# A gated linear attention feeding a gated MLP: the states of the first ten units from one scan each, and units five and six in 64-token chunks

## The chip, the core and the metric

The kernel is one program on 1 core of one Trainium2 chip. The metric is the device time of the program in microseconds (us); lower is better.

The engines have short names below. PE is TensorE's matmul and PEld its weight load. DVE is VectorE, ACT is ScalarE, POOL is GpSimd, and SP is SyncE, which here issues nearly all DMAs.

## The reference

```python
def _attn_ref(q, k, v, alpha):            # 4 x 8 heads, 768 tokens, 48 channels
    for t in range(S):
        state = alpha[:, :, t, :, None] * state + np.einsum('bhd,bhe->bhde', k[:, :, t], v[:, :, t])
        y[:, :, t] = np.einsum('bhd,bhde->bhe', q[:, :, t], state)

def _moe_ref(x, w_gate, w_val, w_out):    # x 3072 x 384, hidden 1536
    gate = 1.0 / (1.0 + np.exp(-(x @ w_gate)))
    val = x @ w_val
    return gate * val @ w_out
```

The output of the recurrence, with the heads side by side, is the `x` of the MLP. All is float32.

## The kernel before

**Units.** The 3072 tokens are cut into six groups `g` of T = 512. In a group, the eight heads are taken as four pairs `p`, so there are 24 units `u = 4 g + p`. A unit computes 512 tokens of two heads. Channels lie on the partitions: one head from partition 0, the other from partition 64.

**One unit.** DVE scans the decays into `G` (L418) and `F` (L422), and `k` and `q` are multiplied by them: L426 and L506 or L638, on DVE or POOL by the tables `KEYS`, `QUERIES` and `WHOLE`. `dec` (L424) holds one decay per chunk. PE transposes the scaled k (L439) and ACT copies it to `kn` (L443). PE computes scores within the chunks, which DVE masks into `A`, and one 48 x 48 addition to the state per chunk. The state is then carried from chunk to chunk: `st[c+1] = st[c] * dec[c] + addition[c]`, one DVE instruction per chunk (L546, L683). POOL multiplies the chunks' states by `dec` into `vs` (L584, L557, L690). PE then forms the outputs from states and scores.

**Two kinds of unit.** Units below `EARLY` = 6 have four chunks of C = 128 tokens (function `unit`). The others have eight chunks of E = 64 (function `late`). The four units of group 0 write their output straight into the PSUM banks `po` (function `in_place`, L597 from states and L602 from scores). Three casts on ACT (L610) and three subtractions on DVE (L611) then make the MLP's input of group 0 from them: `x` in a high and a low part, for k = 0, 1, 2.

**The MLP.** Each group goes through 12 steps, 72 in all. A step has 18 matmuls of 512 columns for gate and value (L245) and 9 into `po` (L746). Between them ACT computes the sigmoid `sg` (L734), DVE the product (L736), ACT its high part `hh` (L737) and DVE the rest `hl` (L738). In group 0, step f also needs weight piece f. It comes as packed words, and for each half of it ACT casts (L376), DVE merges (L379), ACT casts the high part (L382) and DVE subtracts the low part (L390).

**Who sets the order.** Every piece of work is an entry of a plan with an engine, an estimated time and what it reads and writes. For the early program the order on each engine is a table of entry numbers (`ORDER`); behind its end a planner goes by due times. Each engine then runs its own queue in that order. PE starts with 29 matmuls without use (L713).

Of the kernel before, what the change touches and what calls it, by code (L numbers as in the profile page):

```python
# [38 lines left out]
EARLY = 6  # L39
# [166 lines left out]
def act(n):  # L206
    return 0.01 + n / 1065
# [41 lines left out]
def chunked(ctx, tc, rows, vc, vh, vg, weights_in, out, const, ident, flags, weights, within):  # L249
# [64 lines left out]
    r_G0, r_dec = ring("G0", 2, EH), ring("dec", 4, EH)  # L314
# [96 lines left out]
    def decays(u, size, t, inn, tin):  # L411
# [5 lines left out]
        G0, dec = G0[:, 0:nch], dec[:, 0:nch]  # L417
# [11 lines left out]
        return fn, F, decn, dec, gn, G  # L429
# [55 lines left out]
    def unit(u, g, p, t):  # L485
# [6 lines left out]
        if g:  # L492
            vn, v = r_v.next()
            plan.add("sync", (0.475, P * CH * 2 * D * 4 / RATE), after(t["load"], 0.2), lambda: nc.sync.dma_start(
                out=v.rearrange("p c j e -> p (c j e)"), in_=vc[g, p]), writes=[(vn, "v")])
        else:
            vn, vw = r_vg.next()
            plan.add("sync", (0.475, P * CH * GAP * 4 / RATE), t["load"] if u else -1500.0, lambda: nc.sync.dma_start(
                out=vw.rearrange("p c e -> p (c e)"), in_=vg[p]), writes=[(vn, "v")])
            v = vw.rearrange("p c (o e) -> p c o e", o=1)  # L500
            v = [vw[:, :, R * j:R * j + D] for j in range(2)]
        vj = (lambda c, j: v[:, c, j]) if g else (lambda c, j: v[j][:, c])
# [8 lines left out]
        (pkn, pk), *pas = [r_bank.next() for _ in range(3)] if u < NP else [r_gv.next(), r_at.next(), r_at.next()]  # L511
# [26 lines left out]
        st, sn = sts[p], ("st", p)  # L538
        if g:
            plan.add("gpsimd", 0.18, t["G"], lambda: nc.gpsimd.tensor_copy(out=st[:, 0, :], in_=st[:, nch, :]), writes=[sn])  # L540
        else:
            plan.add("gpsimd", 0.08, t["G"], lambda: nc.gpsimd.memset(st[:, 0, :], 0.0), writes=[sn], port=False)

        def states(lo, hi):
            for c in range(lo, hi):
                nc.vector.scalar_tensor_tensor(out=st[:, c + 1, :], in0=st[:, c, :], scalar=dec[:, c:c + 1],  # L546
                                               in1=pk[:, c * D:(c + 1) * D], op0=ALU.mult, op1=ALU.add)

        some = min(t["run"], nch)
        for lo in range(0, nch, some):  # L550
            plan.add("vector", (0.3 * some - 0.12) if some > 1 else 0.19, t["S"], lambda lo=lo: states(lo, min(nch, lo + some)), [decn, pkn], [sn])
        sdn, sd = r_vs.next()
        if not g:
            in_place(p, t, qT, inn, (vn, vw), (an, A), (sdn, sd), (st, sn), (dec, decn))
            return
        sd = sd[:, 0, 0:CH, :]
        plan.add("gpsimd", 0.57, t["sd"], lambda: nc.gpsimd.tensor_tensor(  # L557
            out=sd, in0=st[:, 0:nch], in1=dec.rearrange("p (c o) -> p c o", o=1).broadcast_to([P, nch, D]), op=ALU.mult), [sn, decn], [(sdn, x) for x in range(4)])

        yield  # L560

        pyn, py = r_gv.next()

        def outputs():
            for c in range(nch):
                for j in range(2):
                    cs, r = slice(c * C, (c + 1) * C), slice(R * j, R * j + D)
                    nc.tensor.matmul(out=py[r, cs], lhsT=sd[r, c, :], rhs=qT[r, cs], start=(c == 0), stop=False)  # L568
            for c in range(nch):
                for j in range(2):  # L570
                    cs = slice(c * C, (c + 1) * C)
                    nc.tensor.matmul(out=py[R * j:R * j + D, cs], lhsT=v[:, c, j], rhs=A[:, j, cs],  # L572
                                     start=False, stop=(c == nch - 1))

        plan.add("tensor", (0.46 * nch + 0.15, 0.5), t["out"], outputs, [(vn, "v"), (inn, "q"), *((sdn, x) for x in range(4)), *((an, x) for x in range(4))], [pyn])
        finish(g, p, t, pyn, py)

    def in_place(p, t, qT, inn, vw, A, sd, st, dec):

        (vn, vw), (an, A), (sdn, sd), (st, sn), (dec, decn) = vw, A, sd, st, dec  # L580
# [23 lines left out]
        plan.add("tensor", (1.0, 0.5), t["out"], from_states, [(inn, "q"), *((sdn, x) for x in range(4))], banks)  # L604
# [208 lines left out]
    next(now), next(now)  # L813
# [39 lines left out]
CASTS = ((10, 0),)  # L853
QUERIES = (0, 2)
WHOLE = (4, 5, 6, 8, 9)
KEYS = (0, 1, 2, 3, 4, 8, 10)
# [207 lines left out]
```

## Time and profile before

| | us |
|---|---|
| median of three runs | 513.33 (512.8 to 513.36) |
| the profiled execution's own time | 512.68 |
| its span, first to last instruction | 510.9 |
| busy: PE, DVE, ACT, POOL | 500.6, 328.4, 172.5, 86.1 |

The span is 1.8 us shorter than the time of the same execution. Busy time of PE counts matmuls that overlap in its pipeline, so it is read together with the waits: an engine that is busy and waits for nobody sets the pace.

### The profile page before, as it was taken

The page shows a single profiled execution, that of the slowest core. Times are in us where ns is not written, and L with a number is a line of the kernel's source. Part 1 is how long each engine was busy: PE and PEld are TensorE (multiplying, and loading weights), DVE is VectorE, ACT ScalarE, POOL GpSimd, SP SyncE. Part 2 cuts the span into 40 slices and gives each one's busy share as a digit, 9 for nine tenths or more (in the row PEclk, how much of TensorE's full clock was granted, in tenths as well). Part 3 has the DMA queues.
Part 4 walks back from the last instruction along what each step waited for, and adds up shares of the span by engine and source line. Part 5 has one row for each costly group of instructions (what it writes and reads, how often), then busy time and mean ns, then how long its engine had stood idle before and what let it go on. Part 6 is the DMA issues. An engine that isn't in the chain of part 4 may idle for free.

```text
span 510.9 us, 10507 instructions
## 1 busy us (share of the span) xinstructions
PE 500.6 (98%) x4223; PEld 427.8 (84%) x4223; DVE 328.4 (64%) x639; ACT 172.5 (34%) x330; POOL 86.1 (17%) x110
## 2 busy tenths in 40 slices
PE   8899999999999999999999999999999999999995
PEld 4688888888888888888888888888888888888884
DVE  7999999987747768657558659568665442222221
ACT  2358556553323233223232323222332222311221
POOL 4353111302103303303203113012021010000000
PEclk9999999999999999999999999999999999999998
DMA  8857777851366535725625736436643000100001
GB/s 295 301 205 232 233 260 257 247 154 63 48 146 177 130 86 128 184 61 153 124 55 151 188 67 152 103 89 152 158 96 73 8 10 17 62 1 0 1 1 65
DMA packets 80677, 63.00 MB, mean 123 GB/s; under 512 B 61936, under 2 KB 67312, under 8 KB 80624
## 3 DMA queue, kind: packets, MB, share of 16 engines
q1 hardware_dynamic: 80624, 62.28, 45.2%
q8 instruction: 34, 0.56, 0.5%
q14 instruction: 19, 0.16, 0.1%
HBM read 45.22 MB, written 8.39 MB: 105 GB/s over the span
## 4 chain that ended last, share of the span: by engine, by line
PE 94%; DVE 4%; ACT 1%; DMA 1%; issue 0%; DVEq 0%; SPq 0%; ACTq 0%
PE gv L245 54%; PE po L746 28%; PE gv L702 4%; PE at L654 2%; PE at L660 1%; PE po L602 1%; DVE G L418 1%; PE at L518 1%; PE gv L439 1%; PE po L597 1%; DMA in<-in_rows_dram 1%; DVE raw L379 0%; PE gv L568 0%; PE gv L572 0%; PE gv L523 0%
## 5 line engine op out<-in xcount | busy, mean ns | idle before, releaser
L245 PE MATMUL gv<-x,w 128*128 128x512 f32 x1296 | 300.7, 380 | 0.2 <-DVE hl L738 0.2
L245 PEld LDWEIGHTS gv<-x,w 128*128 128x128 f32 x1296 | 244.4, 189 | 35.2 <-DVE hl L738 0.4
L736 DVE TENSOR_TENSOR gv<-gv,sg 128x512 f32<-128x512 f32 x72 | 50.1, 696 | 127.0 <-PE gv L245 124.1
L746 PE MATMUL po<-hh,w 128*128 128x512 f32 x432 | 111.4, 384 | 0.0
L746 PEld LDWEIGHTS po<-hh,w 128*128 128x128 f32 x432 | 79.9, 189 | 11.8
L734 ACT ACTIVATE sg<-gv 128x512 f32<-128x512 f32 x72 | 43.0, 597 | 127.8 <-PE gv L245 126.6
L737 ACT CAST hh<-gv 128x512 fp32r<-128x512 f32 x72 | 42.2, 586 | 124.1 <-DVE gv L736 114.3
L690 POOL TENSOR_TENSOR vs<-st,dec 64x384 f32<-64x384 f32 x36 | 37.1, 1031 | 270.2 <-PE gv L245 204.3
L738 DVE TENSOR_TENSOR hl<-gv,hh 128x512 fp32r<-128x512 f32 x72 | 49.0, 681 | 24.9 <-ACT hh L737 21.5
L746 PE MATMUL po<-hl,w 128*128 128x512 f32 x216 | 62.8, 381 | 0.0
L746 PEld LDWEIGHTS po<-hl,w 128*128 128x128 f32 x216 | 40.8, 189 | 6.0 <-issue 0.2
L683 DVE SCALAR_TENSOR_TENSOR st<-st,dec,at 128x48 f32<-128x48 f32 x144 | 37.9, 263 | 4.5
L418 DVE TENSOR_TENSOR_SCAN G<-in,d1g 128x512 f32<-128x512 f32 x22 | 31.5, 1431 | 8.7 <-DMA in<-in_rows_dram 8.1
L670 DVE TENSOR_TENSOR A<-at,mask 64x256 f32<-64x256 f32 x72 | 30.2, 420 | 3.5 <-PE at L660 2.8
L422 DVE TENSOR_TENSOR_SCAN F<-in,d1f 128x512 f32<-128x512 f32 x22 | 26.7, 1214 | 0.0
L426 POOL TENSOR_TENSOR in<-in,G 128x512 f32<-128x512 f32 x17 | 22.5, 1323 | 15.8 <-DVE G L418 11.8
L702 PE MATMUL gv<-A,vs 128*48 128x64 f32 x576 | 19.8, 221 | 0.0
L702 PEld LDWEIGHTS gv<-A,vs 128*48 128x48 f32 x576 | 17.1, 123 | 2.4 <-issue 1.3
L464 ACT COPY yt<-gv 128x512 f32<-128x512 f32 x20 | 11.8, 588 | 12.9 <-PE gv L702 11.0
L432 ACT ACTIVATE F<-F 128x512 f32<-128x512 f32 x23 | 14.5, 630 | 4.2 <-DVE in L638 3.7
L654 PEld LDWEIGHTS at<-A,in 48*64 48x64 f32 x576 | 10.0, 134 | 6.0 <-issue 6.0
L382 ACT CAST w<-raw 128x576 fp32r<-128x576 f32 (+1 forms) x16 | 10.4, 652 | 9.7 <-DVE raw L379 9.6
(132 smaller groups left out, 326.3 us busy)
## 6 DMA issues: line engine op xcount, KB each, us to landing
in<-in_rows_dram SPq DMA_DIRECT2D x20, 772.5 KB, 5.8
raw<-in_w_dram SPq DMA_DIRECT2D x14, 577.0 KB, 4.9
first_w<-in_w_dram SPq DMA_DIRECT2D x8, 577.0 KB, 4.9
A<-in SPq DMA_DIRECT2D x36, 128.0 KB, 2.5
out_dram<-raw SPq DMA_DIRECT2D x18, 256.0 KB, 2.3
v<-in_vc_dram SPq DMA_DIRECT2D x20, 192.0 KB, 2.7
way<-G SPq DMA_DIRECT2D x14, 256.0 KB, 3.2
kn<-way SPq DMA_DIRECT2D x56, 64.0 KB, 5.0
```

The lines of the kernel that those rows point to most:

```text
L245: nc.tensor.matmul(out=dst, lhsT=lhs(a, i), rhs=rhs(b, i), start=(n == 0 and i == 0), stop=(n == len(todo) - 1 and i == NK - 1))
L418: plan.add("vector", scan(n), t["G"], lambda: nc.vector.tensor_tensor_scan(out=G[:, ::-1], data0=az[:, n:0:-1], data1=d1g[size], initial=0 ...
L422: plan.add("vector", scan(n), after(t["G"], 0.01), lambda: nc.vector.tensor_tensor_scan(out=F, data0=az[:, 0:n], data1=d1f, initial=0.0, o ...
L670: plan.add("vector", 0.43, t["mask"], lambda pa=pa, j=j, i=i: nc.vector.tensor_tensor(out=A[other[j], j].rearrange("p (c i t) -> p i c t", ...
L683: nc.vector.scalar_tensor_tensor(out=st[:, c + 1, :], in0=st[:, c, :], scalar=dec[:, c:c + 1], in1=pas[c % 2][1][:, T // 2 + c // 2 * D:T ...
L690: plan.add("gpsimd", pool_(EH * D), t["sd"], lambda j=j: nc.gpsimd.tensor_tensor(out=vs[own[j], j], in0=st[own[j], 0:EH], in1=dec[own[j]]. ...
L702: nc.tensor.matmul(out=py[R * j:R * j + D, cs], lhsT=vs[r, j, c, :], rhs=A[r, j, cs], start=True, stop=True)
L734: plan.add("scalar", act(T), first(0.3), lambda: nc.scalar.activation(out=sg, in_=got["g"][1][:, 0:T], func=AF.Sigmoid), [got["g"][0]], [sgn])
L736: plan.add("vector", vec(T), first(0.4), lambda: nc.vector.tensor_tensor(out=pv, in0=pv, in1=sg, op=ALU.mult), [sgn], [pvn])
L737: plan.add("scalar", act(T), first(0.45), lambda: nc.scalar.copy(out=hh, in_=pv), [pvn], [hhn])
L738: plan.add("vector", vec(T), first(0.5), lambda: nc.vector.tensor_tensor(out=hl, in0=pv, in1=hh, op=ALU.subtract), [pvn, hhn], [hln])
L746: nc.tensor.matmul(out=pso_now[m][1][:, 0:T], lhsT=weights.part("o", b, f)[:, m * P:(m + 1) * P], rhs=halves(h[a]), start=(f == 0 and i == ...
```

## The change

- `EARLY` becomes 4. Units 4 and 5 (the fifth and sixth) go through `late` with 64-token chunks.
- Units 0 to 9 (`SCANNED`) get their states in the new function `through`. ACT spreads the chunk decays over the 48 columns (`rep`) and copies the additions out of PSUM (`add`). One DVE scan over 48 x m elements computes all chunks' states already multiplied by `dec` (`sd`); m is 4 for units 0 to 3 and 9 for the others. A zero at the end of `dec` restarts the chain at each column. ACT copies `sd` into `vs`, and POOL forms the state carried to the next unit with one 128 x 48 addition.
- In `in_place` the matmuls from the state of the first chunk, which is zero, are dropped: 9 in place of 12.
- The multiplications of q by F go to POOL for units 2, 6, 8 and 9, and that of k by G for unit 4. Two casts of weight halves go to DVE instead of one.
- The table `ORDER` is new for all engines.

```diff
-EARLY = 6
+EARLY = 4
...
-    r_G0, r_dec = ring("G0", 2, EH), ring("dec", 4, EH)
+    r_G0, r_dec = ring("G0", 2, EH), ring("dec", 4, EH + 1)
+    r_rep, r_add, r_sd = (ring(nm, n, D * (EH + 1), early=[borrow(tag, D * (EH + 1)) for _ in range(2)]) for nm, n, tag in (("rep", 1, "w7"), ("add", 1, "w11"), ("sd", 2, "x1")))
...
+    for nm, t in r_dec.tiles:
+        nc.vector.memset(t[:, EH:EH + 1], 0.0)
...
+    def through(u, g, p, t, nch, decn, ends, banks):
+
+        first = int(g * T % S == 0)
+        m = nch + 1 - first
+        (rn, rep), (dn, add), (sn, sd) = ((nm, x[:, 0:D * m]) for nm, x in (r_rep.next(), r_add.next(), r_sd.next()))
+        chunks = lambda x, lo, hi, by=1: x.rearrange("p (e c) -> p c e", c=m)[:, lo:hi:by]
+        st, stn = sts[p], ("st", p)
+        plan.add("scalar", 0.09 + act(D * m), t["dec"], lambda: nc.scalar.copy(
+            out=rep.rearrange("p (e c) -> p e c", c=m), in_=ends[:, first:nch + 1].rearrange("p (o c) -> p o c", o=1).broadcast_to([P, D, m])), [decn], [rn])
+        if not first:
+            done = EH if u >= EARLY + NP else CH
+            plan.add("gpsimd", 0.23, t["S"], lambda: nc.gpsimd.tensor_copy(out=chunks(add, 0, 1)[:, 0], in_=st[:, done]), [stn], [(dn, "i")])
+        for i, (bn, bank) in enumerate(banks):
+            plan.add("scalar", 0.09 + act(D * nch // len(banks)), t["S"], lambda i=i, bank=bank: nc.scalar.copy(
+                out=chunks(add, 1 - first + i, m, len(banks)), in_=bank), [bn], [(dn, i)])
+        plan.add("vector", 0.09 + scan(D * m), t["S"], lambda: nc.vector.tensor_tensor_scan(
+            out=sd, data0=add, data1=rep, initial=0.0, op0=ALU.add, op1=ALU.mult), [rn, (dn, "i"), *((dn, i) for i in range(2))], [sn], port=True)
+        plan.add("gpsimd", 0.25, t["S"], lambda: nc.gpsimd.tensor_tensor(
+            out=st[:, nch], in0=chunks(add, m - 1, m)[:, 0], in1=chunks(sd, m - 2, m - 1)[:, 0], op=ALU.add), [sn, (dn, "i"), *((dn, i) for i in range(2))], [stn], port=True)
+        return sn, lambda lo, hi: chunks(sd, lo - first, hi - first)
...
-            plan.add("gpsimd", 0.57, t["sd"], lambda j=j, r=r: nc.gpsimd.tensor_tensor(
-                out=sd[r, :, D * j:D * j + D], in0=st[r, 0:CH], in1=dec[r].rearrange("p (c o) -> p c o", o=1).broadcast_to([R, CH, D]), op=ALU.mult),
-                [sn, decn], [(sdn, 2 * j), (sdn, 2 * j + 1)])
+            plan.add("scalar", 0.09 + act((CH - 1) * D), t["sd"], lambda j=j, r=r: nc.scalar.copy(
+                out=sd[r, 1:CH, D * j:D * j + D], in_=some(1, CH)[r]), [sn], [(sdn, 2 * j), (sdn, 2 * j + 1)])
...
-            for c in range(CH):
+            for c in range(1, CH):
...
+        if u < SCANNED:
+            sn, some = through(u, g, p, t, EH, decn, dec, [
+                (pn, bank[:, T // 2:T // 2 + CH * D].rearrange("p (c e) -> p c e", e=D)) for pn, bank in pas])
+            for j in range(2):
+                plan.add("scalar", 0.09 + act(EH * D), t["sd"], lambda j=j: nc.scalar.copy(
+                    out=vs[own[j], j], in_=some(0, EH)[own[j]]), [sn], [(vsn, 2 + j)])
+            yield
+            yield from placed(g, p, t, inn, (an, A), (vsn, vs))
+            return
...
-CASTS = ((10, 0),)
-QUERIES = (0, 2)
-WHOLE = (4, 5, 6, 8, 9)
-KEYS = (0, 1, 2, 3, 4, 8, 10)
+CASTS = ((7, 1), (9, 0))
+QUERIES = (0, 4)
+WHOLE = ()
+KEYS = (0, 1, 2, 3, 8, 10)
...
+SCANNED = 10
```

The new table moves work at three places that matter below. Names are tiles with their buffer numbers; line numbers are those of the respective file, and the form is that of the output.

DVE, from its first scan. Before (`in_81` and `in_82` hold units 0 and 1, `first_w_78` unit 2):

```order
L418 SCALAR_TENSOR_TENSOR G_94<-in_81,d1g_105 128x512
L418 SCALAR_TENSOR_TENSOR first_x_80<-first_w_78,d1g_105 128x512
L420 TENSOR_TENSOR G_98<-G_94,tiny 128x4
L418 SCALAR_TENSOR_TENSOR G_95<-in_82,d1g_105 128x512
L421 RECIPROCAL d1f<-G_98 128x4
L424 TENSOR_TENSOR dec_102<-first_w_78,first_x_80 128x4
L420 TENSOR_TENSOR G_99<-G_95,tiny 128x4
L422 SCALAR_TENSOR_TENSOR F_96<-in_81,d1f 128x512
L420 TENSOR_TENSOR G_98<-first_x_80,tiny 128x4
L426 TENSOR_TENSOR in_81<-in_81,G_94 128x512
L506 TENSOR_TENSOR in_81<-in_81,F_96 128x512
```

And now:

```order
L422 SCALAR_TENSOR_TENSOR G_94<-in_81,d1g_109 128x512
L424 TENSOR_TENSOR G_98<-G_94,tiny 128x4
L428 TENSOR_TENSOR dec_100<-in_81,G_94 128x4
L425 RECIPROCAL d1f<-G_98 128x4
L430 TENSOR_TENSOR in_81<-in_81,G_94 128x512
L426 SCALAR_TENSOR_TENSOR F_96<-in_81,d1f 128x512
L422 SCALAR_TENSOR_TENSOR G_95<-in_82,d1g_109 128x512
L523 TENSOR_TENSOR in_81<-in_81,F_96 128x512
```

Unit 0's k is scaled (L430, L426 before) behind one scan instead of four.

PE, around the first matmuls of the MLP. Before (`w_251` and `w_448` are weight pieces 0 and 1, `at` and the rows of L518 unit 4's scores):

```order
L597 MATMUL po_129<-first_w_77,vs_93 32x128 x12
L602 MATMUL po_129<-first_w_75,first_w_74 32x128 x16
...
L518 MATMUL at_122<-in_81 128x128
L518 MATMUL at_123<-in_81 128x128
L245 MATMUL gv_125<-x_115,w_251 128x512 x3
L245 MATMUL gv_124<-x_115,w_448 128x512 x3
L245 MATMUL gv_125<-x_115,w_251 128x512 x6
```

And now (`w_318` and `w_483` are weight pieces 0 and 1, L464 the transposes of unit 4):

```order
L245 MATMUL gv_129<-x_119,w_318 128x512 x3
L464 MATMUL gv_128<-ident,in_81 128x128 x4
L245 MATMUL gv_130<-x_119,w_318 128x512 x3
L575 MATMUL po_133<-first_w_77,vs_93 32x128 x9
L580 MATMUL po_133<-first_w_75,first_w_74 32x128 x16
L245 MATMUL gv_129<-x_119,w_318 128x512 x3
L245 MATMUL gv_130<-x_119,w_318 128x512 x3
L245 MATMUL gv_128<-x_119,w_483 128x512 x9
L245 MATMUL gv_130<-x_119,w_318 128x512 x3
L245 MATMUL gv_129<-x_119,w_318 128x512 x3
L632 MATMUL at_126<-A_90,in_81 64x64
```

Twelve matmuls of the MLP now stand ahead of the nine that first need all of `x`, some of them ahead of unit 3's outputs (L575, L580), and unit 4's scores (L632) come after.

ACT, around the first `hh`. Before:

```order
L734 ACTIVATE sg_116<-gv_125 128x512
L382 CAST w_551<-raw_86 128x576
L432 ACTIVATE F_97,flags<-F_97 128x512
L432 ACTIVATE first_x_80,flags<-first_x_80 128x512
L376 CAST first_w_77<-first_w_76 128x576
L737 CAST hh_118<-gv_126 128x512
```

And now (L442 spreads decays, L448 copies additions):

```order
L442 COPY rep_104<-dec_100 128x432
L379 CAST first_w_78<-raw_86 128x576
L726 ACTIVATE sg_120<-gv_129 128x512
L385 CAST w_585<-first_w_79 128x576
L385 CAST w_585<-raw_86 128x576
L726 ACTIVATE sg_120<-gv_128 128x512
L729 CAST hh_122<-gv_130 128x512
L379 CAST first_w_77<-first_w_76 128x576
L448 COPY add_105<-at_127 128x4x48
L448 COPY add_105<-at_126 128x4x48
```

The new copies of unit 4's state stand in one queue with the MLP's `sg` and `hh` and the casts of the weights.

## Rows read from the trace of the kernel before

**Rows 1.** The page: busy time, and the chain by engine.

```profile
PE 500.6 (98%) x4223; PEld 427.8 (84%) x4223; DVE 328.4 (64%) x639; ACT 172.5 (34%) x330; POOL 86.1 (17%) x110
...
PE 94%; DVE 4%; ACT 1%; DMA 1%; issue 0%; DVEq 0%; SPq 0%; ACTq 0%
```

**Rows 2.** Waits of PE: total us, times, longest us.

```profile
PE po L597 <- POOL vs L584: 1.4, 1, 1.4
...
PE gv L245 <- DVE hl L738: 0.2, 1, 0.2
```

**Rows 3.** Busy us by stretch: PE, PEld, DVE, ACT, POOL, then granted clock, DMA, GB/s.

```profile
3.81:35.00 31.19, 28.17 (x422) 20.85 (x421) 30.90 (x69) 12.45 (x29) 12.51 (x21) 1.00 0.82 293
35.00:60.00 25.00, 25.00 (x183) 20.80 (x179) 23.96 (x42) 16.85 (x30) 6.86 (x7) 1.00 0.75 237
60.00:85.00 25.00, 24.76 (x276) 20.92 (x273) 24.32 (x49) 14.85 (x28) 5.04 (x4) 1.00 0.77 245
85.00:110.00 25.00, 25.00 (x206) 21.52 (x205) 23.62 (x46) 15.06 (x26) 4.88 (x6) 1.00 0.80 236
```

**Rows 4.** Timeline of PE: start, us from first start to last end, what.

```profile
35.54 8.04 PE L245 MATMUL gv<-x,w 128*128 128x512 f32 x36
...
43.94 1.08 PE L568 MATMUL gv<-in,vs 48*48 48x128 f32 x16
...
45.97 0.66 PE L439 MATMUL gv<-ident,in 128*128 128x128 f32 x4
...
48.71 0.56 PE L523 MATMUL gv<-v,kn 128*48 128x48 f32 x16
49.21 2.21 PE L245 MATMUL gv<-x,w 128*128 128x512 f32 x9
...
51.56 1.16 PE L518 MATMUL at<-in 48*128 48x128 f32 x16
52.65 6.09 PE L245 MATMUL gv<-x,w 128*128 128x512 f32 x27
```

**Rows 5.** The same view, at a unit with 64-token chunks.

```profile
94.61 0.69 PE L654 MATMUL at<-A,in 48*64 48x64 f32 x32
...
95.59 2.21 PE L245 MATMUL gv<-x,w 128*128 128x512 f32 x9
...
98.59 1.10 PE L702 MATMUL gv<-A,vs 128*48 128x64 f32 x32
99.63 0.48 PE L746 MATMUL po<-hh,w 128*128 128x512 f32 x1
```

**Rows 6.** Timeline of DVE.

```profile
3.81 1.23 DVE L418 TENSOR_TENSOR_SCAN G<-in,d1g 128x512 f32<-128x512 f32 x1 [1.94 <-DMA in<-in_rows_dram]
4.95 1.20 DVE L418 TENSOR_TENSOR_SCAN first_x<-first_w,d1g 128x512 f32<-128x512 f32 x1
...
34.33 0.25 DVE L546 SCALAR_TENSOR_TENSOR st<-st,dec,gv 128x48 f32<-128x48 f32 x1
34.50 0.75 DVE L390 TENSOR_TENSOR w<-first_w,w 128x576 fp32r<-128x576 f32 x1
...
36.86 0.68 DVE L611 TENSOR_TENSOR x<-po,x 128x512 fp32r<-128x512 f32 x1
37.46 0.91 DVE L379 SCALAR_TENSOR_TENSOR first_w<-first_w,top 128x576 uint32<-128x576 uint32 x1
```

**Rows 7.** Groups of ACT, whole span: busy us, mean ns, idle before.

```profile
L763 ACT COPY raw<-po 128x256 f32<-128x256 f32 x2 | 0.8, 377 | 2.9 <-PE po L746 2.9
L428 ACT COPY starts<-G 128x8 f32<-128x8 f32 (+1 forms) x23 | 4.5, 201 | 15.9 <-DVE G L418 15.9
L443 ACT COPY kn<-gv 128x512 f32<-128x512 f32 x7 | 4.1, 589 | 11.6 <-PE gv L439 9.2 <-PE at L523 2.4
```

**Rows 8.** The same view, DVE.

```profile
L670 DVE TENSOR_TENSOR A<-at,mask 64x256 f32<-64x256 f32 x72 | 30.2, 420 | 3.5 <-PE at L660 2.8
...
L379 DVE SCALAR_TENSOR_TENSOR raw<-raw,top 128x576 uint32<-128x576 uint32 (+1 forms) x10 | 8.8, 884 | 0.2
```

More of the change, by code (lines that the diff above doesn't have):

```diff
@@ L416, in decays @@
         (gn, G), (fn, F), (g0n, G0), (decn, dec) = r_G.next(), r_F.next(), r_G0.next(), r_dec.next()
-        G0, dec = G0[:, 0:nch], dec[:, 0:nch]
+        G0, ends = G0[:, 0:nch], dec[:, EH - nch:EH + 1]
+        dec = ends[:, 0:nch]
         plan.add("vector", scan(n), t["G"], lambda: nc.vector.tensor_tensor_scan(
@@ L428, in decays @@
         plan.add("scalar", 0.14, t.get("first", t["flag"]), lambda: nc.scalar.copy(out=starts[:, u, 0:nch], in_=G[:, 0:n:size]), [gn], [("start", u)])
-        return fn, F, decn, dec, gn, G
+        return fn, F, decn, ends, gn, G
+    def through(u, g, p, t, nch, decn, ends, banks):
[17 more added lines that the diff above has]
+        return sn, lambda lo, hi: chunks(sd, lo - first, hi - first)
     def bound(u, t, fn, F):
@@ L491, in unit @@
                 out=tin[:, lo:hi], in_=rows[g, p, :, lo:hi]), writes=[(inn, m) for m in marks])
[L492 to L502, printed above, removed]
+        vn, vw = r_vg.next()
+        plan.add("sync", (0.475, P * CH * GAP * 4 / RATE), t["load"] if u else -1500.0, lambda: nc.sync.dma_start(
+            out=vw.rearrange("p c e -> p (c e)"), in_=vg[p]), writes=[(vn, "v")])
         kT, qT = tin[:, A_K:A_Q], tin[:, A_Q:WIDTH]
@@ L508, in unit @@
         bound(u, t, fn, F)
-        (pkn, pk), *pas = [r_bank.next() for _ in range(3)] if u < NP else [r_gv.next(), r_at.next(), r_at.next()]
+        (pkn, pk), *pas = [r_bank.next() for _ in range(3)]
         knn, kn = turn(t, inn, kT, pkn, pk)
@@ L522, in adds @@
                 for j in range(2):
-                    nc.tensor.matmul(out=pk[R * j:R * j + D, c * D:(c + 1) * D], lhsT=kn[:, c, R * j:R * j + D], rhs=vj(c, j),
+                    nc.tensor.matmul(out=pk[R * j:R * j + D, c * D:(c + 1) * D], lhsT=kn[:, c, R * j:R * j + D], rhs=vw[:, c, R * j:R * j + D],
                                      start=True, stop=True)
@@ L535, in unit @@
         yield
[L538 to L580, printed above, removed]
+        in_place(u, p, t, qT, inn, (vn, vw), (an, A), through(u, 0, p, t, nch, decn, dec, [(pkn, pk[:, 0:nch * D].rearrange("p (c e) -> p c e", e=D))]))
+    def in_place(u, p, t, qT, inn, vw, A, states):
+        (vn, vw), (an, A), (sn, some), (sdn, sd) = vw, A, states, r_vs.next()
@@ L594, in from_states @@
         def from_states():
-            for c in range(CH):
+            for c in range(1, CH):
                 for i in range(3):
-                    nc.tensor.matmul(out=at(i, c), lhsT=sd[0:GAP, c, 32 * i:32 * i + 32], rhs=qT[0:GAP, c * C:(c + 1) * C], start=(c == 0), stop=False)
+                    nc.tensor.matmul(out=at(i, c), lhsT=sd[0:GAP, c, 32 * i:32 * i + 32], rhs=qT[0:GAP, c * C:(c + 1) * C], start=(c == 1), stop=False)
         def from_scores(j):
@@ L602, in from_scores @@
                     nc.tensor.matmul(out=at(i, c), lhsT=vw[:, c, lo:lo + 32], rhs=A[:, j, c * C:(c + 1) * C], start=False, stop=(c == CH - 1 and (i, j) != (1, 0)))
-        plan.add("tensor", (1.0, 0.5), t["out"], from_states, [(inn, "q"), *((sdn, x) for x in range(4))], banks)
+        plan.add("tensor", (0.75, 0.5), t["out"], from_states, [(inn, "q"), *((sdn, x) for x in range(4))], banks)
         for j in range(2):
@@ L690, in late, with placed @@
             plan.add("gpsimd", pool_(EH * D), t["sd"], lambda j=j: nc.gpsimd.tensor_tensor(
-                out=vs[own[j], j], in0=st[own[j], 0:EH], in1=dec[own[j]].rearrange("p (c o) -> p c o", o=1).broadcast_to([R, EH, D]), op=ALU.mult),
+                out=vs[own[j], j], in0=st[own[j], 0:EH], in1=dec[own[j], 0:EH].rearrange("p (c o) -> p c o", o=1).broadcast_to([R, EH, D]), op=ALU.mult),
                 [sn, decn], [(vsn, 2 + j)])
         yield
+        yield from placed(g, p, t, inn, (an, A), (vsn, vs))
+    def placed(g, p, t, inn, A, vs):
+        (an, A), (vsn, vs) = A, vs
         pyn, py = r_gv.next()
@@ L705, in late @@
         finish(g, p, t, pyn, py)
+        yield from ()
     wz = ident.bitcast(BF16)[:, 0:P]
@@ L812, in chunked @@
     now, following = begin(NP), None
-    next(now), next(now)
+    for _ in range(3 if NP >= EARLY else 2):
+        next(now)
     for s in range(NG * NF):
@@ L859 @@
     "tensor": (
[7 rows of a table removed]
[7 rows of a table added]
     ),
     "vector": (
[9 rows of a table removed]
[8 rows of a table added]
     ),
     "scalar": (
[5 rows of a table removed]
[6 rows of a table added]
     ),
     "gpsimd": (
-        111, 141, 5, 3, 2, 0, 1, 81, 53, 73, 59, 58, 4, 86, 87, 133, 116, 117, 320, 147, 146, 502, 438, 312, 325, 365, 379, 367, 618, 415, 384, 486, 479,
-        447, 448, 512, 694, 511, 767, 840, 607, 696, 621, 752, 697, 620,
+        5, 2, 3, 72, 0, 56, 101, 4, 1, 130, 305, 312, 374, 141, 367, 322, 326, 83, 388, 112, 432, 392, 425, 486, 493, 449, 453, 554, 510, 514, 623, 779, 611,
+        618, 627, 703, 764, 781,
     ),
     "sync": (
[4 rows of a table removed]
[4 rows of a table added]
     ),
```

50 rows, old and new, of the table ORDER are left out of this document.

## Prediction

> **What bounds the kernel now.** I read the page first. PE is busy for 98% of the span, and the chain that ended last runs on PE for 94% of it [rows 1]. Busy time alone proves little, since matmuls overlap, so the waits come next: PE's longest waits are 1.4 us for POOL's states and 0.7 us or less for the rest, all but one in the start, and the MLP's gate and value matmuls waited 0.2 us once in the whole run [rows 2]. From about 35 us on, PE therefore never stands still for long, and the time is the moment at which the MLP gets going plus all the PE work that is left. The windows then say who could hold PE up: until 110 us DVE is busy 94 to 99% of each stretch, ACT 40 to 67%, POOL 20 to 40% [rows 3]. DVE prepares the weights of group 0, so it is the engine that PE would wait for next. The granted clock is full in all these stretches.
>
> **The change on PE.** A unit with 128-token chunks costs PE, apart from the transposes, which stay, 1.09 us of scores (51.56 to 52.65), 0.50 of additions (48.71 to 49.21) and 2.03 of outputs (43.94 to 45.97), 3.62 together [rows 4]. A unit with 64-token chunks costs 0.98 (94.61 to 95.59) and 1.04 (98.59 to 99.63), 2.02 together [rows 5]. One matmul of 512 columns takes 0.216 us: 27 of them last 3.88 us longer than 9 [rows 4].
>
> I compare the two programs at one point each. Before, the MLP starts at 35.54 [rows 4]; units 0 to 3 are done then, unit 4 lacks its outputs (2.03), and unit 5 all of its 3.62: 5.65 of work. In the new order I take the first of the nine matmuls that come first behind the twelve early ones (the listing of the change on PE). There, units 0 to 3 are done too, units 4 and 5 lack 2.02 each, 4.04 together, and 12 matmuls of the MLP are already through. What is left is less by 5.65 - 4.04 = **1.6 us** and by 12 x 0.216 = **2.6 us**. The rest of the program is the same on PE.
>
> **When that point comes.** Those nine matmuls need the third low part of `x`. DVE has it before at 37.46, counting from its first scan at 3.81 [rows 6], and stands idle for 0.3 us in between [rows 3]. So I take that stretch of DVE's queue and put the differences of the new one in. They are: 20 state instructions out, at 0.17 each from start to start (34.33 to 34.50), -3.4; one multiplication of k, one of q and one mask out, at 0.60 (36.86 to 37.46 is another of that size), -1.8; one 512-wide scan more, at 1.14 (3.81 to 4.95), +1.1 [rows 6]; small ones of 128x8, +0.2 by count and size; and four scans over 192 elements.
>
> The trace has no scan that short. It costs no less than 192/512 of 1.14, 0.43, and no more than 1.14. It is the same operation on the same kind of tile, so I take the lower end with a little of a fixed part, 0.46: +1.8. The sum is -2.1, and the low part comes at 35.4. The first three of the nine matmuls need only high parts, so the point itself lies 3 x 0.216 earlier, at 34.8: **0.7 us** before 35.54. If the scans cost the upper end, it comes 4 x 0.68 = 2.7 later.
>
> PE must be there as well. Its own work up to that point is five transposes of about 0.4, four times 1.09 and 0.50, four times about 2.7 for outputs (three quarters of the matmuls from states) and 2.6 of MLP, about 22 us. From its first transposes at 6 us or so that leaves 6 us for waits, more than what it had between 3.81 and 35, where it was not busy for 3.0 us [rows 3].
>
> Together: 0.7 + 2.6 + 1.6 = 4.9 us less.
>
> **What may be given back.** Behind that point PE arrives earlier at every weight piece, and DVE must keep up. I count both queues in the new order. DVE from 35.4 to the second half of piece 9: 16 merges at 0.81 (884 ns less the overlap of 0.07) [rows 8], 17 subtractions at 0.67 (34.50 to 35.17 for the same size), 17 products at 0.60, 8 scans at 1.14 [rows 6], 16 masks at 0.42 [rows 8], four scans over 432 elements at 0.97 (432/512 of 1.14), and 3.2 of others, 57.4 us: ready at 92.8. PE from 34.8 to the value matmuls of step 9: 230 x 0.216, five times 0.98, four times 1.04 and four transposes, 60.3 us: there at 95.1. The margin is 2.3 us. The same count gives 1.9 at piece 4 and 0.7 at piece 2. The sums have no idle time in them; DVE's before was 1.0 + 0.7 + 1.4 = 3.1 us between 35 and 110 [rows 3], 2.2 by 93. That eats the margin and no more, so I charge nothing for it.
>
> The thinnest place is the first `hh`. DVE's product is ready at 35.4 + 4.2 = 39.6 by the same durations; ACT, in the new order, does a second `sg` and then `hh`, 0.59 each by its copies of 512 [rows 7], and PE reaches `po` at 34.8 + 24 x 0.216 + 0.98 = 40.9, when `hh` is ready at 40.8. One ACT instruction that is late there (0.6 to 0.9) is paid in full, and such places repeat. I charge **0.8 us**, an estimate of one such instruction.
>
> The new copies on ACT have no row of their own shape. One of 192 to 432 elements costs between 0.20 (8 elements) and 0.59 (512); 256 take 0.38 [rows 7]; I take 0.3 to 0.5. A 64-token unit then adds `rep` 0.5, two `add` 0.3, two into `vs` 0.45: 2.0 us. Four of them in the 50 us from 35 to 85 bring ACT from 31.7 [rows 3] to 40 of 50, which still fits. At the upper price it is 43.
>
> The moved multiplications cost DVE less and POOL more, but POOL loses the multiplications by `dec`. For the stretch from 35 to 110, where POOL was busy 16.8 us [rows 3], I count the new list at about the same, so POOL stays hidden behind work that has several us of lead; without that lead, one late multiplication would cost up to its 1.3 us.
>
> The four dropped matmul groups (3 of 12 per unit, about 0.25 us each) lie in the start, where PE has room, and are counted there as nothing. The four extra memsets on DVE run before the first load has landed.
>
> A rule to weigh: while POOL reads, DVE's new scans may stand. In the trace, a merge with two inputs in SBUF takes 884 ns on average [rows 8] where the subtraction of the same size takes 0.75 [rows 6], so something does stretch it. The Trainium skill, "SBUF — State Buffer", section "SBUF: two separate sides", says that a DVE instruction with two SBUF inputs and a GpSimd instruction that reads SBUF exclude each other for a whole instruction. The old state instructions read their addition from PSUM; the new scans read both inputs from SBUF. By that rule the sum would come out 0.7 us higher, at 509.9; the trace agrees so far that merges are stretched, and no row here shows a scan that stood still.
>
> **The sum.** 4.9 less 0.8 is 4.1 us. Against the profiled execution that is 512.68 - 4.1 = 508.6; the median of the runs lies 0.65 above that execution, so I forecast **509.2 us**.
>
> **The rivals.**
>
> *DVE comes late.* The four short scans stand on the way to `x` for 1.8 us, in a stretch where POOL is busy 12.5 of 31 us [rows 3]. If each stands still for that share, 0.7 is lost before the MLP; the four longer ones lose another 0.9 at a POOL share of 22%. With the merges stretched too, and margins of 0.7 to 2.3, PE waits about 2 us more: 511.2. For it speaks that DVE has no room; against it that POOL's total does not grow.
>
> *The short scans cost as much as long ones.* Then the start moves by 2.0 the wrong way, and 4.1 - 2.7 = 1.4 us remain: 511.9. This is also what is left when the change does not speed up the start as it is ordered to. The scan's time per element in one row speaks against it.
>
> *Slower: ACT's queue holds the MLP.* Six units with 64-token chunks put 2.0 us each into the queue that also holds `sg` and `hh`. If PE waits 1.1 us at each for an `hh` behind copies that themselves wait for a scan, 6.6 us are lost: 4.9 - 6.6 is +1.7, so 515.0. From 0.8 us per unit on, nothing of the gain is left. For it speaks the margin of 0.1 at the first `hh`; against it ACT's free third of the time.
>
> **How the numbers follow.** A measurement of this kernel cannot tell less than about 0.2%, 1.0 us, from no change. The forecast, with its own range of 507.5 to 510.6, gets 0.62. DVE late gets 0.15 (it holds the rule above as a part), dear scans 0.08, ACT 0.09, and a gain and a loss that cancel within 1 us 0.06. Faster are the forecast, DVE late and most of the third: 0.83. Same are the last case and some of the third: 0.08. Slower is ACT: 0.09. The range goes from 507.3 (512.68 - 4.9 = 507.8 with nothing given back, and 0.5 below it for scans and copies at their lower ends) to 512.2, which holds the forecast and the two smaller gains.
>
> **What the profile after would show.** Right: the first MLP matmul before 31 us, the third low part of `x` near 35.4, scans of 192 near 0.5 us and of 432 near 1.0, blocks of about 2.0 us for units 4 and 5, and no wait of PE over 1 us behind 36 us. Wrong: PE waiting for DVE's subtractions of the weights (margins), for `hh` from ACT, or for POOL's q. The forecast fails as a whole if PE's idle time between 35 and 110 us grows by more than 4 us.

## The result and the profile after

The changed kernel takes 508.36 us (median of four runs, 508.01 to 509.44). The kernel before took 513.35 beside it. The ratio is 0.9894, with a 95% interval of 0.9853 to 0.9936. Six more runs in a later session, in which the kernel before took 513.06, have a median of 508.86 and a ratio of 0.9910 (0.9885 to 0.9935). So the change is worth 4.2 to 5.0 us. The ten runs lie between 508.01 and 509.51, with a median of 508.6, which is the base for the experiments below. The first four experiments ran in a session in which the kernel before took 512.65, 0.4 to 0.7 us less than beside the base, so a difference smaller than that from the base says little by itself.

The profiled execution took 509.44 us, with a span of 507.6: 3.24 us less than the one of before (512.68). All rows below are from it, so the accounting is made against 3.24.

Busy time and the chain, from the page (against [rows 1]):

```profile
PE 497.5 (98%) x4263; PEld 425.3 (84%) x4263; DVE 323.0 (64%) x597; ACT 194.9 (38%) x375; POOL 85.7 (17%) x103
...
PE 90%; DVE 3%; DMA 2%; ACT 2%; issue 1%; SPq 0%; DVEq 0%
```

ACT has 22 us more to do and PE's share of the chain has gone from 94 to 90%: the chain passes from PE to other engines more often. The waits of PE's weight loads say to whom (total us, times, longest us; against [rows 2]):

```profile
PEld gv L693 <- ACT vs L659: 2.3, 5, 0.7
...
PEld po L738 <- ACT hh L729: 0.8, 3, 0.4
PEld gv L464 <- issue: 0.8, 1, 0.8
PEld gv L245 <- ACT kn L468: 0.7, 2, 0.5
```

The outputs of the 64-token units (L693) wait five times for ACT's copies into `vs` (L659). By stretch (columns as in [rows 3]):

```profile
3.81:35.00 31.19, 29.62 (x390) 21.95 (x389) 30.75 (x56) 20.43 (x49) 9.50 (x10) 1.00 0.86 307
35.00:60.00 25.00, 24.78 (x261) 20.84 (x260) 22.86 (x39) 20.75 (x38) 9.11 (x11) 1.00 0.80 246
60.00:85.00 25.00, 24.39 (x284) 20.35 (x283) 22.97 (x38) 18.75 (x33) 4.31 (x4) 1.00 0.87 245
85.00:110.00 25.00, 24.33 (x202) 20.70 (x201) 23.49 (x35) 19.24 (x37) 5.84 (x7) 1.00 0.76 240
```

Between 35 and 110 us PE is now not busy for 1.50 us, where it was 0.24 [rows 3]; DVE's idle time has grown to 5.7 us from 3.1, and ACT's work to 58.7 us from 46.8. Behind 35 us PE now waits for ACT more than for DVE.

The start of the MLP, on PE's timeline (against [rows 4]):

```profile
28.27 0.92 PE L245 MATMUL gv<-x,w 128*128 128x512 f32 x3
29.02 0.60 PE L464 MATMUL gv<-ident,in 128*128 128x128 f32 x4
29.38 0.89 PE L245 MATMUL gv<-x,w 128*128 128x512 f32 x3
30.20 0.86 PE L575 MATMUL po<-first_w,vs 112*32 112x128 f32 x18
30.88 1.92 PE L580 MATMUL po<-first_w,first_w 128*32 128x128 f32 x32
32.73 4.80 PE L245 MATMUL gv<-x,w 128*128 128x512 f32 x21
37.46 0.70 PE L632 MATMUL at<-A,in 48*64 48x64 f32 x32
37.98 0.54 PE L638 MATMUL at<-v,kn 64*48 64x48 f32 x32
38.45 2.21 PE L245 MATMUL gv<-x,w 128*128 128x512 f32 x9
```

Three, three and six of the 21 are the twelve early matmuls. The first of the nine that need all of `x` is the seventh of the 21 and starts at 34.13 (32.73 + 0.32 for the first of the block + 5 x 0.216).

The third low part of `x` and the first scans for states, on DVE's timeline (against [rows 6]):

```profile
33.46 0.69 DVE L589 TENSOR_TENSOR x<-po,x 128x512 fp32r<-128x512 f32 x1 [0.19 <-ACT x L588]
...
43.36 0.17 DVE L428 TENSOR_TENSOR dec<-in,G 128x8 f32<-128x8 f32 x1
43.44 1.05 DVE L450 TENSOR_TENSOR_SCAN sd<-add,rep 128x432 f32<-128x432 f32 x1
44.41 0.83 DVE L382 SCALAR_TENSOR_TENSOR raw<-raw,first_w 128x576 uint32<-128x576 uint32 x1
```

A scan of 432 elements holds DVE for 0.97 us, as taken. The new copies on ACT (groups; busy us, mean ns; against [rows 7]):

```profile
L659 ACT COPY vs<-sd 64x384 f32<-64x384 f32 x12 | 10.8, 904 | 6.0 <-DVE sd L450 5.9
...
L448 ACT COPY add<-at 128x192 f32<-128x192 f32 x13 | 6.4, 527 | 0.0
...
L442 ACT COPY rep<-dec 128x432 f32<-128x432 f32 x6 | 3.3, 551 | 0.0
```

`rep` takes 0.55 us, near the 0.5 that was taken, but an `add` takes 0.53, where 0.3 was put down, and one half of `vs` 0.90, where 0.45 was. What that does to PE, on its timeline at units 4 to 7:

```profile
45.97 1.54 PE L693 MATMUL gv<-A,vs 128*48 128x64 f32 x32
47.60 1.13 PE L738 MATMUL po<-hh,w 128*128 128x512 f32 x4
...
60.76 1.33 PE L693 MATMUL gv<-A,vs 128*48 128x64 f32 x32
62.02 0.70 PE L632 MATMUL at<-A,in 48*64 48x64 f32 x32
...
78.83 0.31 PE L693 MATMUL gv<-A,vs 128*48 128x64 f32 x2
79.64 1.09 PE L693 MATMUL gv<-A,vs 112*48 112x64 f32 x30 [0.49 <-ACT vs L659]
80.66 0.70 PE L632 MATMUL at<-A,in 48*64 48x64 f32 x32
...
94.45 1.10 PE L693 MATMUL gv<-A,vs 128*48 128x64 f32 x32 [0.28 <-ACT vs L659]
```

At units 4 and 6 PE starts with the first half of `vs` and stands before the second. From the block's start to the next instruction it takes 1.63, 1.26 and 1.83 us at units 4 to 6, where 1.03 is its time without a wait; at unit 7 it waits before the block.

### The profile page after: what moved, and what is told of

Its sections match the earlier page's. It is cut to its first block, busy times and chain, and to the rows that moved or that the text cites. A ratio compares the mean times of both kernels' runs of the same rounds, so it can differ in the third digit from the quotient of the medians.

```text
span 507.6 us, 10590 instructions
## 1 busy us (share of the span) xinstructions
PE 497.5 (98%) x4263; PEld 425.3 (84%) x4263; DVE 323.0 (64%) x597; ACT 194.9 (38%) x375; POOL 85.7 (17%) x103
## 4 chain that ended last, share of the span: by engine, by line
PE 90%; DVE 3%; DMA 2%; ACT 2%; issue 1%; SPq 0%; DVEq 0%
PE gv L245 52%; PE po L738 27%; PE gv L693 4%; PE at L632 2%; PE po L580 1%; PE at L638 1%; DMA v<-in_vc_dram 1%; DMA x<-yt 1%; DVE G L422 1%; PE po L575 1%; DMA in<-in_rows_dram 1%; ACT vs L659 1%; ACT w L385 0%; DVE w L393 0%; PE at L535 0%
## 5 line engine op out<-in xcount | busy, mean ns | idle before, releaser
L677 POOL TENSOR_TENSOR vs<-st,dec 64x384 f32<-64x384 f32 x28 | 27.9, 998 | 228.4 <-PE gv L245 227.3
L648 DVE TENSOR_TENSOR A<-at,mask 64x256 f32<-64x256 f32 x80 | 33.5, 419 | 4.8 <-PE at L638 3.3
L670 DVE SCALAR_TENSOR_TENSOR st<-st,dec,at 128x48 f32<-128x48 f32 x112 | 29.7, 265 | 3.6
L426 DVE TENSOR_TENSOR_SCAN F<-in,d1f 128x512 f32<-128x512 f32 x22 | 27.8, 1262 | 0.2
L430 POOL TENSOR_TENSOR in<-in,G 128x512 f32<-128x512 f32 x18 | 24.1, 1336 | 19.4 <-DVE G L422 12.1
L693 PE MATMUL gv<-A,vs 112*48 112x64 f32 (+1 forms) x640 | 22.9, 222 | 0.9 <-ACT vs L659 0.8
L693 PEld LDWEIGHTS gv<-A,vs 112*48 112x48 f32 (+1 forms) x640 | 19.5, 123 | 3.9 <-ACT vs L659 2.3
L632 PEld LDWEIGHTS at<-A,in 48*64 48x64 f32 x640 | 11.2, 134 | 5.9 <-issue 5.6
L616 POOL TENSOR_TENSOR in<-in,F 128x512 f32<-128x512 f32 x6 | 10.0, 1664 | 34.8 <-DVE F L426 34.8
```

The lines of the kernel that those rows point to most:

```text
L426: plan.add("vector", scan(n), after(t["G"], 0.01), lambda: nc.vector.tensor_tensor_scan(out=F, data0=az[:, 0:n], data1=d1f, initial=0.0, o ...
L648: plan.add("vector", 0.43, t["mask"], lambda pa=pa, j=j, i=i: nc.vector.tensor_tensor(out=A[other[j], j].rearrange("p (c i t) -> p i c t", ...
L693: nc.tensor.matmul(out=py[R * j:R * j + D, cs], lhsT=vs[r, j, c, :], rhs=A[r, j, cs], start=True, stop=True)
```

## Experiments

Times are medians.

**Is PE or DVE the bound of the start?** Two kernels add work, one on each engine.

```diff
-            for c in range(1, CH):
+            for c in range(CH):
                 for i in range(3):
-                    nc.tensor.matmul(..., start=(c == 1), stop=False)
+                    nc.tensor.matmul(..., start=(c == 0), stop=False)
```

> The twelve dropped matmuls from zero states (3 in each of units 0 to 3, about 0.25 us per unit, 1.0 us together) are done again; the result is the same. Theory A, the step of the prediction: PE has room in the start and the MLP waits for DVE's third low part of x, so the time stays within 0.3 us of 508.4. Theory B: behind 15 us PE runs from one block to the next with gaps of 0.2 us, so the start is bound by PE's own work, and the time rises by about 1.0 us.

It took 510.11 us (ratio to before 0.9938, 0.9914 to 0.9962), 1.5 above the base. The blocks of L575 last 0.91 us instead of 0.69 from start to start, 0.88 more for the four, and the block of 21 matmuls starts at 34.21, 1.48 later; the rest of that is a late load at the very start of this one execution (0.55). DVE now waits for PE through ACT:

```profile
34.94 0.69 DVE L589 TENSOR_TENSOR x<-po,x 128x512 fp32r<-128x512 f32 x1 [0.76 <-ACT x L588]
```

Theory B holds: PE's own work in the start counts in full. What the medians show beyond the 0.88 stays open.

```diff
-        plan.add("vector", ..., lambda: nc.vector.tensor_tensor_scan(out=sd, data0=add, ...), ...)
+        plan.add("vector", ..., lambda: [nc.vector.tensor_tensor_scan(out=sd, data0=add, ...)
+                                         for _ in range(2 if u < EARLY else 1)], ...)
```

> The state scans of units 0 to 3 (192 elements, 0.46 us from start to start) are each done twice, with the same result. Theory A, the step of the prediction: DVE's queue sets when the third low part of x comes, so it comes 1.8 us later than 34.15, and the time rises by about 1.8 us, less the slack of PE's filler matmuls. Theory B: PE is the bound of the start, the low part has slack, and the time rises by less than 0.6 us.

It took 511.0 us (0.9959, 0.9943 to 0.9974), 2.4 above the base. The second scans hold DVE for 2.37 us together. The third low part starts at 35.9, 2.4 later, and PE, which did not wait there before, now stands before the last outputs of unit 3:

```profile
31.18 0.86 PE L575 MATMUL po<-first_w,vs 112*32 112x128 f32 x18
32.69 1.94 PE L580 MATMUL po<-first_w,first_w 128*32 128x128 f32 x32 [0.65 <-DVE first_w L548]
34.56 4.80 PE L245 MATMUL gv<-x,w 128*128 128x512 f32 x21
```

Theory A holds too, but for some room on DVE: the block of 21 matmuls starts 1.83 later, and the profiled execution is 1.80 longer than that of the changed kernel. The start is one chain that passes from DVE to PE and back with little slack: work added on PE is paid in full, work added on DVE but for about half a microsecond.

**What do the copies into `vs` cost?**

```diff
-                plan.add("scalar", ..., t["sd"], lambda j=j: nc.scalar.copy(
-                    out=vs[own[j], j], in_=some(0, EH)[own[j]]), ...)
+                plan.add("scalar", ..., t["sd"], lambda j=j: [nc.scalar.copy(
+                    out=vs[own[j], j], in_=some(0, EH)[own[j]]) for _ in range(2)], ...)
```

> Every copy of sd into vs (L659, 0.90 us each, two per unit, units 4 to 9) is done twice on ACT with the same result, so each unit's vs is complete 1.8 us later. Theory A: PE stands in front of the outputs of these units until the copies are there, with no slack, and the time rises by 1.8 us at the four or five units where PE waited already, 6 to 10 us in all. Theory B: what PE loses there it would lose later to DVE's weights anyway, and the time rises by less than 2 us.

It took 519.63 us (1.0126, 1.0097 to 1.0154), 11.0 above the base: as much as twelve copies of 0.90, above theory A's range. PE's wait for `vs`, matmuls alone without the weight loads, is 7.2 us (0.8 in the changed kernel), 1.7 more went to its clock (see the last section), 1.6 to one wait for `sg`, and the rest to small ones. So only 6.4 of the 11.0 us is PE standing for `vs`; that the total is twelve copies' worth is not shown to be more than chance.

**Can another engine take one of the two?** `MOVED` names one half for each of units 4 to 8, and the entry moves in the table, behind the same scan.

```diff
+                en = "gpsimd" if MOVED.get(u) == j else "scalar"
-                plan.add("scalar", ...)
+                plan.add(en, ..., lambda j=j, en=en: (nc.scalar.copy if en == "scalar" else nc.gpsimd.tensor_copy)(...))
```

> The second of the two copies of sd into vs goes to POOL for units 4 to 8, so that both halves are copied at once. Theory A: the waits of PE for vs (0.33, 0.69, 0.45 us and the slow blocks of L693) vanish, and the time falls by 1.5 to 2.5 us. Theory B: a copy on POOL takes longer than two on ACT, or stretches DVE's instructions, and the time stays within 0.5 us of 508.4 or rises.

It took 507.31 us (0.9883, 0.9857 to 0.9909), 1.3 below the base. A copy on POOL takes 1.07 us on average, more than the 0.90 on ACT, but beside it, not behind it. The outputs of unit 6, which took 1.83 us, on PE's timeline (lines behind L659 are one further in this file):

```profile
78.09 1.10 PE L694 MATMUL gv<-A,vs 128*48 128x64 f32 x32
79.12 0.70 PE L632 MATMUL at<-A,in 48*64 48x64 f32 x32
```

They take 1.03, and no wait of L694 for `vs` is left. The session is not the cause: from the first matmul that needs all of `x` to the end, this execution takes 471.5 us, and the two profiled ones of the changed kernel 473.5 and 473.1. Theory A holds, at its price by this stretch (1.5 to 1.9), a little below it by the medians.

The same with DVE's copy in place of POOL's:

> The second of the two copies of sd into vs goes to DVE for units 4 to 8, right behind its scan. Theory A: PE's waits of 1.6 us come from the two ACT copies in a row and DVE has room for five copies of 0.5 us or so, so the time falls by 1 to 1.6 us, as with the copy on POOL. Theory B, the margins of the prediction (DVE 2.3, 1.9 and 0.7 us ahead of PE): five copies, 2.5 us together, use up what DVE has, PE waits for weights or products instead, and the time stays within 0.5 us of the changed kernel or rises.

It took 508.01 us (0.9896, 0.9873 to 0.9920), 0.6 below the base. DVE's copy takes 0.51 us. The waits for `vs` are gone here too, but PE waits elsewhere:

```profile
PEld po L739 <- ACT hh L730: 1.5, 3, 0.9
```

That was 0.8. DVE's products come later, so ACT's `hh` does. By the medians, half of what the copy on POOL brings is lost; by the stretch from the first matmul that needs all of `x`, 471.9 us, only 0.3 us. The result lies between the theories: DVE has some room, but the copies cost waits elsewhere.

**Why does a copy of 384 elements take 0.90 us?**

```diff
-                    out=vs[own[j], j], in_=some(0, EH)[own[j]]), ...
+                    out=vs[own[j], j].rearrange("p c e -> p e c"), in_=some(0, EH)[own[j]].rearrange("p c e -> p e c")), ...
```

> The copies of sd into vs run in the other order: chunk inside, column outside, so that they read runs of 8 elements that lie together and write with a stride of 48 elements; before they read with a stride of 9 and write without one. Theory A: the stride of the read makes these copies dear (0.90 us for 384 elements where 512 without strides take 0.59), so they fall to about 0.5 us, PE's waits for vs shrink, and the time falls by 1 to 1.5 us. Theory B: a stride on either side, or the half of the partitions, costs the same, so they stay at 0.85 to 1.0 us and the time within 0.4 us.

The copies still take 881 ns, as theory B has it, but the kernel took 507.5 us (0.9887, 0.9863 to 0.9911; 507.32 to 508.66), 1.1 below the base and 1.4 below the changed kernel in the same session, against theory B: the time is theory A's, without its cause. The profiled execution is the slowest of the six. In it unit 6's wait is 0.2 us in place of 0.7, and two other waits of the changed kernel are gone (0.55 before L464, 0.26 for `kn`), but there is a new one of 1.0 us for `hl`. Why the waits move while the copies last as long stays open.

The next kernel (one run, 509.91 us) measures the copy by itself. It writes into a tile that nobody reads:

```diff
+    narrow, wide = (lambda x: x[:, 0:D * EH].rearrange("p (c e) -> p c e", e=D)), (lambda x: x.rearrange("p (e c) -> p c e", c=EH + 1)[:, 0:EH])
+    for i in range(3):
+        for n, (r, src, dst) in enumerate(((slice(0, P), narrow, narrow), (slice(0, P), wide, narrow), (slice(0, P), narrow, wide),
+                                           (slice(0, R), narrow, narrow), (slice(0, R), wide, narrow), (slice(R, P), wide, narrow))):
+            plan.add("scalar", ..., lambda r=r, src=src, dst=dst: nc.scalar.copy(out=dst(rep)[r], in_=src(sd)[r]), [sn], [rn])
```

> Six more copies on ACT, three times each, in the quiet second half: sd into a tile that nobody reads any more, 384 elements in each partition, with 128 partitions without strides, with a stride of 9 elements in the read, with that stride in the write; then with 64 partitions without strides, with the stride in the read in the lower half, and in the upper. The output stays the reference's. Theory A: a stride makes the copy dear: the second, third, fifth and sixth take 0.9 us, the first and fourth 0.45. Theory B: half of the partitions makes it dear: the last three take 0.9, the first three 0.45. Theory C: neither alone, all below 0.6 us, and the copies in the kernel are dear because of what runs beside them.

The first set, on ACT's timeline, in the order of the list:

```profile
155.88 0.50 ACT L834 COPY rep<-sd 128x384 f32<-128x384 f32 x1
...
156.41 0.92 ACT L834 COPY rep<-sd 128x384 f32<-128x384 f32 x1
...
158.24 2.38 ACT L834 COPY rep<-sd 128x384 f32<-128x384 f32 x3
...
161.12 0.92 ACT L834 COPY rep<-sd 64x384 f32<-64x384 f32 x1
```

The row of three holds the write with a stride (0.91), the 64 partitions without (0.51) and with a stride in the read (0.90). The other two sets differ by 0.03 at most. Theory A holds: a stride on either side costs ACT 0.4 us for 384 elements, about 1 ns for each; the number of partitions costs nothing. This is also why the order inside the copy changes nothing in its duration: one side has the stride in either order. The Trainium skill, "SBUF — State Buffer", section "Door 1: The DMA port swizzle", says that accesses which go to a new 16-byte line each time pay a penalty, so that four fp32 are the stride that is free. ACT's copies, with a stride of 9 or 48 fp32, agree; DVE's copy with a stride of 9 (0.51 us) is not shown to pay.

**How much is the table, how much the program?** Without `ORDER`, the planner sets the whole order.

```diff
-ORDER = {
-    "tensor": (
...
-}
+ORDER = {}
```

> The changed kernel without the table of the early order: the planner's own costs and due times set the order everywhere. Theory A: the gain lies in what the program does (64-token units, scans) and the table is worth a few us, so the time is 511 to 516 us. Theory B: the gain lies in the table, so that without it the changed kernel is not faster than the kernel before without its table; the kernel before_planner gives the number to hold against it. Either way a time of 512 to 525 us is expected.

> The kernel before without its table of the early order: the planner's own costs and due times set the order everywhere. It is the number to hold against the changed kernel without its table, 521.2 us. Theory A: the change is worth what it is for any order, 4 to 5 us, so this one takes 525 to 527 us. Theory B: the gain lies in the new table, so this one takes 521 us or less.

The changed kernel without its table took 521.22 us (1.0161, 1.0128 to 1.0194), the kernel before without its own 522.96 (1.0196, 1.0159 to 1.0233). The difference is 1.7 us, with intervals that overlap. The kernel before lands midway between the theories (521 or less, 525 to 527), so the new program is worth at most a part of the gain by itself, and the rest is the table's: the old table brings 9.9 us, the new one 12.6 (521.22 - 508.6).

A third kernel, also without a table, has `SCANNED = 4` in place of 10:

> The changed kernel without its table, and with scans for units 0 to 3 alone: units 4 to 9 carry their states with eight DVE instructions each and POOL's multiplications, as before. Theory A: the scans take 1.0 us of DVE where the chains take 1.4 to 2.1, and DVE is what PE waits for without the table, so this one is 3 to 6 us slower than 521.2. Theory B: ACT's copies cost the unit as much as the chain and the multiplications did, so the time stays within 2 us of 521.2.

It took 524.16 us (1.0212, 1.0179 to 1.0246), 2.9 above the same with ten scans, just short of theory A. With an interval that overlaps that of the kernel before without its table (522.96), it shows no gain of the 64-token units under this planner unless the scans come with them.

**A version faster than both.** Copy on POOL and the other order inside the copies together:

> Both edits that came out faster than the changed kernel: the second copy of sd into vs on POOL for units 4 to 8, and the copies with the chunk inside. Theory A: the two gains have the same cause, PE's waits for vs, which are gone with the copy on POOL alone, so the time stays within 0.4 us of 507.3. Theory B: the order inside the copies brings something of its own, and the time falls to 506.3 to 506.9.

It took 507.26 us (0.9878, 0.9854 to 0.9902), the same as with POOL's copy alone. Theory A holds. They are 5.3 and 5.8 us below the kernel before beside them.

## Why the prediction was right, point by point

The forecast was 509.2 us for the median and 508.6 for the profiled execution. The medians were 508.36 and 508.86, the two profiled executions of this kernel 509.44 and 508.99. The mechanism was right and the range held, but two terms were off, in opposite directions: the start gained 0.7 us more than was said, and 1.2 us more was given back. That the total came so near is in part luck.

**The point of comparison was said to come at 34.8; it came at 34.13.** So the start gained 1.4 us, not 0.7. DVE finished the third low part at 34.15, where 35.4 was said. From the start of the first scan to the start of this subtraction its queue took 33.05 us before and takes 29.69 now: 3.4 less, where -2.1 was worked out. The short scans were right: four hold DVE for 1.87, where 1.8 was taken. The 20 state instructions were mis-sized: they held DVE for 3.92 us, not 20 x 0.17 = 3.4, since the row used was one that stood alone, and those that followed each other took 0.20 to 0.26 each. So were the multiplications of k (0.94 less, not 0.6, since one of those before had lasted 0.93) and the small instructions (0.2 less, not 0.2 more).

The step itself was also incomplete. PE did not wait for the low part: it needed it three matmuls after 34.13, 0.6 us after it was there. PE's own matmuls, three of them without use, fill the time from 14.74 to 34.13 without a wait on its timeline. So "where PE has room" did not hold, and "The four dropped matmul groups [...] are counted there as nothing" was wrong: they are 0.88 us on PE's timeline. DVE's queue counts as well (1.8 of the 2.37 us that the scans done twice add).

**Twelve early matmuls, 2.6 us, and 64-token units, 1.6 us.** Both stand: twelve matmuls lie ahead of the point, and a block takes 0.98 and, without a wait, 1.03.

**Given back: 0.8 us was charged, 2.0 was paid.** The blocks of L693 for units 4, 5 and 6 last 1.63, 1.26 and 1.83 us, together 1.63 more than three of 1.03, and unit 7's starts 0.35 late. Of these 2.0 us, 0.27 at unit 4 is the first `hh` (behind the same copies) and 0.23 at unit 5 a mask of DVE's; the other 1.5 is `vs`. The step that failed is "two into `vs` 0.45", from rows without strides [rows 7]: they take 0.90 each, so a unit costs ACT 0.55 + 2 x 0.53 + 2 x 0.90 = 3.4 us, not 2.0. It was mostly the second half of `vs` that was late, not the first `hh`. That this is the cause is shown by POOL's copy, which takes the waits and 1.3 us away; the copies done twice show that ACT has no room for more of them. It is the mechanism of the rival that had ACT's queue hold the MLP, with `vs` in place of `hh`, at a third of its price. With 0.98 of scores, units 4 and 5 took 2.6 and 2.2 us, not the "about 2.0" that was to show.

With the measured terms, 1.4 + 2.6 + 1.6 - 2.0 = 3.6 us. Waits of 0.55 us before L464 and 0.26 for `kn`, against one of 0.31 for `hl` in the kernel before, take off 0.5: 3.1, against 3.24 between the two profiled executions.

**DVE's margins** held: behind 36 us PE waited for DVE 0.2 us at one mask, and otherwise only briefly for `hl`. The copy on DVE shows that they are narrow. One reading was incomplete: PE's longest wait before was not the 1.4 us named but 1.6 us for `ident` at the very start; it is there after the change too and alters nothing. **POOL** was busy 19.3 us between 35 and 110 us, more than the 16.8 said, and stayed hidden.

**The rule weighed for POOL and DVE** agrees with this trace, but it did not decide. What counts is who starts first:

```profile
85.23 0.94 DVE L382 SCALAR_TENSOR_TENSOR raw<-raw,top 128x576 uint32<-128x576 uint32 x1
85.44 1.83 POOL L616 TENSOR_TENSOR in<-in,F 128x512 f32<-128x512 f32 x1 [6.84 <-DVE F L426]
...
95.09 1.27 POOL L430 TENSOR_TENSOR in<-in,G 128x512 f32<-128x512 f32 x1 [1.21 <-DMA raw<-in_w_dram]
95.19 1.85 DVE L382 SCALAR_TENSOR_TENSOR first_w<-first_w,top 128x576 uint32<-128x576 uint32 x1 [0.23 <-ACT top L379]
...
155.83 1.28 POOL L430 TENSOR_TENSOR in<-in,G 128x512 f32<-128x512 f32 x1
155.96 2.23 DVE L426 TENSOR_TENSOR_SCAN F<-in,d1f 128x512 f32<-128x512 f32 x1
```

The merge at 95.19 and the scan of 512 elements at 155.96 start just behind a multiplication of POOL's and last 1.85 and 2.23 us, where 0.75 to 0.95 and 1.22 are usual. The merge at 85.23 starts first: it lasts as usual, and POOL's multiplication takes 1.83 in place of 1.27. Scans also stood still in the kernel before, all behind 170 us (1.80 us at 193.57, for one), outside the rows that the prediction read. The four short scans took 0.54 to 0.56 us each, since none started behind a reading of POOL's that had more than 0.12 us to go. So the 0.7 us of the rule was not paid.

## What to carry to other kernels

Price a moved operation by a row with the same strides, not only the same size: here the strides took the copies from 0.50 to 0.90 us, and PE waited 1.5 us for them. Where two engines hand work to each other with little slack, count the work removed from either. A helper's two halves that a consumer needs together belong on two engines, even if the second is slower.

## What the runs showed of the hardware

PE's clock fell once behind a wait. In the kernel with the copies done twice, PE stood for 2.1 us before unit 7's outputs, and the granted clock went from full to half (1.2 GHz) about 0.5 us after it had begun again, for 3.4 us (windows; the last three numbers are granted clock, DMA share and GB/s):

```profile
98.00:100.00 2.00, 0.50 (x3) 0.09 (x1) 1.28 (x2) 1.96 (x3) 0.79 (x2) 1.00 0.55 119
100.00:101.00 1.00, 0.39 (x14) 0.39 (x16) 0.00 (x0) 1.00 (x2) 0.68 (x1) 1.00 0.96 397
101.00:102.00 1.00, 1.00 (x26) 0.91 (x21) 0.65 (x1) 0.79 (x2) 0.00 (x0) 0.57 0.19 74
102.00:103.00 1.00, 1.00 (x40) 0.95 (x40) 0.11 (x1) 0.83 (x2) 0.00 (x0) 0.50 0.03 8
103.00:104.00 1.00, 1.00 (x41) 0.91 (x35) 0.71 (x2) 0.83 (x3) 0.00 (x0) 0.50 0.00 0
104.00:105.00 1.00, 1.00 (x4) 0.85 (x5) 0.72 (x2) 1.00 (x2) 0.00 (x0) 0.72 0.97 124
```

The sum of what is missing from 1.00 in those four rows is 1.7 us. Waits of 1.5 to 1.7 us at units 4 to 6, and of 1.6 us at 143, left the clock full.

On the same 384 elements without strides ACT's copy takes 0.50 us; with them ACT takes 0.90, DVE 0.51 and POOL 1.07. DVE's products of 512 elements without strides take 0.69 (L616), which is 0.52 for 384 in proportion: by these rows the stride costs ACT much and DVE little, though no run has DVE's copy without a stride.
